# A three-network kernel on one core: the prologue rewritten, odd row tiles stored with 128 rows

## The chip, the cores and the metric

The kernel runs on one core of one Trainium2 chip. The metric is device time in microseconds (us) of one launch; the median of several runs counts.

The core has five engines that run at once and wait for one another by semaphores: PE (matmul; PEld is its weight load), DVE (vector), ACT (activation), POOL (GpSimd) and SP, which here does nothing but issue DMA transfers. Each engine takes its instructions in program order, so an instruction that waits holds up all that stand behind it on its engine.

## What is computed

Three networks in a row, all in float32 with some split into two parts of lower precision (a high and a low part) that are multiplied apart:

```python
kv = np.einsum('bhsd,bhse->bhde', k, v)            # 8 batches, 8 heads, 576 x 64
out = np.einsum('bhsd,bhde->bhse', q, kv)
out = out / np.sqrt(np.mean(out * out, -1, keepdims=True) + 1e-06) * g_norm
x = heads of out side by side                       # 8 x 576 x 512
u = x + real(fft(fft(x, axis=1), axis=2))
un = (u - mean) / sqrt(var + 1e-06)                 # over the last axis
x = u + max(un @ w1a, 0) @ w2a                      # 512 -> 2048 -> 512
u = x + (x.T @ U @ V).T                             # over the 576 rows, rank 32
return u + max(u @ w1b, 0) @ w2b
```

The weights come as 64-bit words that the kernel itself turns into float32 ("conversion" below).

## The kernel before

**Stages.** `tile_fused_kernel` is written in program order (`manual_schedule`), so the order of the code is the order on every engine. The *prologue* (L1232 to the line `early.clear()`) does batch 0 up to its normalised, transposed rows. Then come nine times 16 steps `n` of the first two-layer network: *block* j = n // 16 holds 512 rows, and the steps of block j also carry batch j + 1 through the attention, the DFT and the stores (`batch_tasks`, by step). The rest, from step 144, is a fast matrix product for the second network, which the change doesn't touch.

**A step of block 0.** `emit_l1(n)` is 12 matmuls of 128x512 (L223 to L225, with the weight's high part `w1h` and low part `w1l`), then come the eight passes of `emit_l2(n - 1)` (L244, needs the activation `g` of the step before). In the first block the steps also convert the weights: `w_load` (L102) starts a 512 KB transfer into one of four raw buffers, `w_mags` (`conv_0`, L113 and L114, ACT) takes it apart, `conv_a` (L122, L123) and `conv_b` (L128, L130) make the float32 tile on DVE, for every second tile with L130 on POOL. `w_next` then loads into the buffer that `conv_b` has just read. `split_w1` makes `w1h` on ACT (L198) and `w1l` on POOL (L199), or on DVE for steps in `on_dve`. ACT takes `w_mags` ahead of the next `g`.

**The prologue's path.** `load_first` brings k, v and q of batch 0 in two halves of four heads. `t_kv` multiplies k and v, `t_o0` multiplies by q half by half and takes the squares and sums (ten half tiles), `t_norm` scales. `t_fold_s`, `t_fold_e`, `t_fold_h`, `t_fold_l` fold the rows for a half-size DFT, `c` being one of three row chunks, `p` the even or odd part. `t_s1` is the DFT over the rows (PE, then `t_s1_out`: high part `y` on ACT, low part `y` on DVE), `t_s2` the DFT over the columns, three chunks in the order 2, 0, 1, each with seven DVE or ACT operations behind it that leave u in `x`. `f_stats` and `f_rs` make the mean and the reciprocal deviation, `f_norm` the normalised rows, `f_tr` the transpose into `xh` and `xl`, which `emit_l1(0)` reads. `keep_warm(n)` is n matmuls of 128x128 on the identity.

**Stores.** `t_u_out(b, c)` stores u to memory, two transfers for each chunk: the even rows (L549; 128, 128, 33 of them) and the odd rows (L551; 127, 128, 32: the first of chunk 0 is left out, since row 288 is an even one). The SP engine issues all transfers of the kernel in program order; a transfer's issue waits until the one eight places before it in the round has ended.

Of the kernel before, what the change touches and what calls it, by code (L numbers as in the profile page):

```python
# [45 lines left out]
def kernel(ctx: ExitStack, tc: tile.TileContext, qT, kvm, gn, w1a, w2a, w1b, w2b,  # L46
# [354 lines left out]
    def t_o0(k, half):  # L401
        s = st[0]
        g, c, m = OT[k]
        if k + half == 0:
            s["x"] = at.tile([C, 2, 3, DM], F32, tag="xpn", name="x0")
            s["sq"] = at.tile([C, 5, DM], F32, tag="slot_b", name="sq0")
            s["ss"] = whole(at, [C, 5, H], F32, "ss0", "ss", 2)
        ps = side_bank(f"o0_{k}_{half}")[:m, 0:256]
        cols, hs = slice(256 * half, 256 * half + 256), slice(4 * half, 4 * half + 4)
        for j in range(2):  # L410
            nc.tensor.matmul(out=ps[:, 128 * j:128 * j + 128], lhsT=s["q"][:, 2 * half + j, C * k:C * k + m],
                             rhs=kvbd[:, 2 * half + j, :], start=True, stop=True)
        sq = s["sq"][:m, k, cols]
        nc.scalar.activation(out=sq, in_=ps, func=AF.Square)
        heads = lambda v: v.rearrange("p (h d) -> p h d", d=D)
        nc.vector.tensor_tensor(out=heads(s["x"][:m, g, c, cols]), in0=heads(ps),
                                in1=gnb[:m].unsqueeze(1).to_broadcast([m, 4, D]), op=ALU.mult)
        ss = s["ss"][:m, k, hs]
        nc.vector.reduce_sum(out=ss, in_=heads(sq), axis=AX.X)
        nc.vector.tensor_scalar(out=ss, in0=ss, scalar1=1.0 / D, scalar2=EPS, op0=ALU.mult, op1=ALU.add)  # L420
        nc.gpsimd.tensor_tensor(out=ss, in0=ss, in1=nhalf[:m, 0:4], op=ALU.pow)

    def t_norm(b, k):
        s = st[b]
        g, c, m = OT[k]
        xv = s["x"][:m, g, c].rearrange("p (h d) -> p h d", d=D)
        rs = s["ss"][:m, k]
        if b == 1 or b == 0 and k in (1, 3):
            for h in range(8):
# [128 lines left out]
    def load_first():  # L558
        kv = at.tile([128, 2, KC, DM], F32, tag="slot_a", name="kv0")
        q = whole(at, [128, 4, NQ], F32, "q0", "slot_c")  # L560
        for half in range(2):
# [3 lines left out]
            if half == 0:
                nc.sync.dma_start(out=gnb, in_=gn)
            j = slice(2 * half, 2 * half + 2)
            nc.sync.dma_start(out=q[:, j], in_=qT[0][:, j])
# [662 lines left out]
    with tc.manual_schedule():  # L1231
# [20 lines left out]

        keep_warm(15)
        t_kv(0, 0)
        t_o0(0, 0)
        t_o0(1, 0)
        t_kv(0, 1)
        for k in range(2, 5):
            t_o0(k, 0)
        for k in range(5):  # L1260
            t_o0(k, 1)
        keep_warm(40)
        for k in (0, 1, 3):
            t_norm(0, k)
        for p in range(2):
            for c in range(3):
                t_fold_s(0, c, p)
                t_fold_e(0, c, p)
                t_fold_h(0, c, p)
                if p and c < 2:  # L1270
                    round_table(2, c)
                if p == 0:
                    if c == 0:
                        round_table(0, 0)
                    if c < 2:
                        t_norm(0, 2 * c + 2)
                if c:
                    t_fold_l(0, c - 1, p)
            t_fold_l(0, 2, p)
            round_table(2 - (not p), 2 * p)  # L1280
            if p == 0:
                for e in range(2):
                    t_s1_mm(0, 0, e)
                t_kve_mm(1, 0)
        for e in range(2):
            t_s1_out(0, 0, e)
# [248 lines left out]
```

## Time and profile before

| | us |
|---|---|
| median of 3 runs | 1778.59 (1778.1 to 1779.77) |
| the profiled execution | 1778.37 |
| its span, first to last instruction | 1776.6 |
| PE busy | 1740.6 (98%) |
| DVE, ACT, POOL busy | 1179.6, 833.6, 466.7 |
| DMA, share of 16 engines (q1) | 53.5% |

PE is the engine that sets the time. What PE is not busy is read by stretches: the prologue ends, and the first matmul of step 0 starts, at 61.23 us; block 0 goes to about 192 us. The granted clock is given as a share of full speed, 1.00 for 2.4 GHz and 0.50 for 1.2 GHz, so a stretch between the two shows a mean. DMA share 0.06 is one of the 16 DMA engines.

### The profile page before, as it was taken

Reading aid. Unit: us, or ns where it says so; the run is one execution under the profiler, and the core shown is the slowest. Engines: PE = TensorE matmul, PEld = TensorE weight load, DVE = VectorE, ACT = ScalarE, POOL = GpSimd, SP = SyncE. Lnnn points to the kernel's source line nnn. Section 1 sums busy time; section 2 is a strip of 40 time slices with the busy share of each in tenths; the row PEclk is TensorE's granted clock in tenths of the full one; section 3 lists DMA queues with packets and bytes.
Section 4 is the critical chain, followed back from the end, with each engine's and each line's share of the span. In section 5 each row is a group of like instructions: output and inputs, shape, how many; then the busy total and the mean of one; then the engine's idle time right before and its main releaser. Section 6 shows DMA issues by size and latency. Waiting matters only on the chain.

```text
span 1776.6 us, 23224 instructions
## 1 busy us (share of the span) xinstructions
PE 1740.6 (98%) x8206; PEld 1427.1 (80%) x8206; DVE 1179.6 (66%) x1927; ACT 833.6 (47%) x1601; POOL 466.7 (26%) x368
## 2 busy tenths in 40 slices
PE   7898999999999999999999999999999999999999
PEld 7666688888888888888888878878888888888877
DVE  5687777868677686765676666448835863594285
ACT  5575344444444344343446564456445534552253
POOL 2164445464534545443322223000000000000000
PEclk9999999999999999999999999999999999999999
DMA  8554315051432505203368864767776776777675
GB/s 327 188 193 148 127 36 195 6 183 54 157 135 96 174 24 206 86 20 114 102 234 307 312 224 168 233 175 247 239 241 182 236 257 194 220 227 236 188 217 188
DMA packets 130292, 315.23 MB, mean 177 GB/s; under 512 B 20592, under 2 KB 23424, under 8 KB 128512
## 3 DMA queue, kind: packets, MB, share of 16 engines
q1 hardware_dynamic: 130176, 313.75, 53.5%
q8 instruction: 65, 1.06, 0.2%
q14 instruction: 51, 0.42, 0.1%
HBM read 238.83 MB, written 74.86 MB: 177 GB/s over the span
## 4 chain that ended last, share of the span: by engine, by line
PE 83%; DVE 3%; DMA 3%; ACT 1%; issue 0%; SPq 0%; POOL 0%; ACTq 0%; DVEq 0%; POOLq 0%
PE y L1129 10%; PE yy L1209 10%; PE h L225 7%; PE h L223 7%; PE h L224 6%; PE acc L252 6%; PE acc L254 6%; PE acc L253 6%; PE z L1209 5%; PE zz L1129 5%; PE w L1209 3%; PE z L1129 3%; PE o L383 2%; DMA raw<-in_w2b 1%; PE pt L825 1%; DVE w2l L209 1%
## 5 line engine op out<-in xcount | busy, mean ns | idle before, releaser
L199 POOL TENSOR_TENSOR w1l<-w,w1h 128x512 fp32r<-128x512 f32 x147 | 200.0, 1361 | 402.8 <-ACT w1h L198 384.9
L223 PE MATMUL h<-xl,w1h 128*128 128x512 f32 x576 | 231.9, 403 | 4.8 <-DVE xl L679 2.6
L225 PE MATMUL h<-xh,w1l 128*128 128x512 f32 x576 | 226.2, 393 | 2.3 <-POOL w1l L199 2.3
L224 PE MATMUL h<-xh,w1h 128*128 128x512 f32 x576 | 225.7, 392 | 0.0
L252 PE MATMUL acc<-w2h,gl 128*128 128x512 f32 x524 | 206.1, 393 | 0.2 <-DVE gl L233 0.2
L254 PE MATMUL acc<-w2h,gh 128*128 128x512 f32 x524 | 204.3, 390 | 0.0
L253 PE MATMUL acc<-w2l,gh 128*128 128x512 f32 x524 | 204.2, 390 | 0.0
L1129 PE MATMUL y<-xv,v 128*128 128x512 f32 x768 | 191.8, 395 | 2.7 <-ACT g L1066 2.7
L232 ACT ACTIVATE gh<-h 128x512 fp32r<-128x512 f32 x147 | 87.5, 595 | 222.9 <-PE h L225 220.7
L1066 ACT ACTIVATE g<-y 128x512 f32<-128x512 f32 x128 | 76.6, 598 | 211.5 <-PE y L1129 211.5
L1129 PEld LDWEIGHTS y<-xv,v 128*128 128x128 f32 x768 | 143.7, 188 | 38.2 <-ACT g L1066 4.5
L233 DVE SCALAR_TENSOR_TENSOR gl<-h,gh 128x512 fp32r<-128x512 f32 x147 | 100.7, 685 | 87.6 <-ACT gh L232 87.3
L209 DVE TENSOR_TENSOR w2l<-w,w2h 128x512 fp32r<-128x512 f32 x147 | 139.1, 946 | 27.1 <-ACT w2h L208 26.7
L223 PEld LDWEIGHTS h<-xl,w1h 128*128 128x128 f32 x576 | 108.8, 189 | 27.3 <-ACT w1h L198 2.8
L225 PEld LDWEIGHTS h<-xh,w1l 128*128 128x128 f32 x576 | 108.7, 189 | 27.0 <-POOL w1l L199 3.5
L224 PEld LDWEIGHTS h<-xh,w1h 128*128 128x128 f32 x576 | 108.9, 189 | 22.2 <-issue 1.7
L252 PEld LDWEIGHTS acc<-w2h,gl 128*128 128x128 f32 x524 | 98.4, 188 | 22.1 <-DVE gl L233 2.5
L254 PEld LDWEIGHTS acc<-w2h,gh 128*128 128x128 f32 x524 | 98.4, 188 | 20.5
L253 PEld LDWEIGHTS acc<-w2l,gh 128*128 128x128 f32 x524 | 98.5, 188 | 19.7
L198 ACT ACTIVATE w1h<-w 128x512 fp32r<-128x512 f32 x160 | 99.8, 624 | 26.2 <-DVE w L130 20.8
L208 ACT ACTIVATE w2h<-w 128x512 fp32r<-128x512 f32 x147 | 91.7, 624 | 34.3 <-PE acc L254 30.7
L1060 DVE TENSOR_TENSOR g<-zz,g 128x512 f32<-128x512 f32 x64 | 44.2, 691 | 93.1 <-ACT g L1066 80.1
(243 smaller groups left out, 3678.8 us busy)
## 6 DMA issues: line engine op xcount, KB each, us to landing
v<-wv_d SPq DMA_DIRECT2D x224, 512.0 KB, 3.9
wv_d<-vo SPq DMA_DIRECT2D x112, 256.0 KB, 2.7
kve<-in_kvm SPq DMA_DIRECT2D x40, 256.0 KB, 6.1
x_d<-x2o SPq DMA_DIRECT2D x36, 256.0 KB, 2.1
x2f<-x_d SPq DMA_DIRECT2D x36, 256.0 KB, 5.2
outT<-o SPq DMA_DIRECT2D x36, 256.0 KB, 2.9
q<-in_qT SPq DMA_DIRECT2D x7, 1220.0 KB
raw<-in_w1b SPq DMA_DIRECT2D x16, 512.0 KB
```

The lines of the kernel that those rows point to most:

```text
L198: nc.scalar.activation(out=ah, in_=a, func=AF.Copy)
L199: (nc.vector if n in on_dve else nc.gpsimd).tensor_tensor(out=al, in0=a, in1=f32(ah), op=ALU.subtract)
L209: nc.vector.tensor_tensor(out=cl, in0=c, in1=f32(ch), op=ALU.subtract)
L223: nc.tensor.matmul(out=h, lhsT=ah[:, kc, :], rhs=xl[:, kc, :], start=(kc == 0), stop=False)
L224: nc.tensor.matmul(out=h, lhsT=ah[:, kc, :], rhs=xh[:, kc, :], start=False, stop=False)
L225: nc.tensor.matmul(out=h, lhsT=al[:, kc, :], rhs=xh[:, kc, :], start=False, stop=(kc == 3))
L233: nc.vector.scalar_tensor_tensor(out=gl, in0=h, scalar=0.0, in1=f32(gh), op0=ALU.max, op1=ALU.subtract)
L252: nc.tensor.matmul(out=a, lhsT=gl[:, tt], rhs=ch, start=s, stop=False)
L253: nc.tensor.matmul(out=a, lhsT=gh[:, tt], rhs=cl, start=False, stop=False)
L254: nc.tensor.matmul(out=a, lhsT=gh[:, tt], rhs=ch, start=False, stop=e)
L1129: nc.tensor.matmul(out=dst, lhsT=w[:, c], rhs=r[:, k], start=p in (0, 1, 3) and k + n == 0, stop=k == 1 and n == 2, skip_group_check=True)
L1209: nc.tensor.matmul(out=dst[mp], lhsT=w[:, c], rhs=r, start=p in (0, 1, 6, 3) and i + n == 0, stop=i == 7 and n == 2, skip_group_check=True)
```

## The change

- `t_o0` is gone. Batch 0 uses `t_o`, as the others do, over whole heads (five tiles); `load_first` brings k and v in halves, then q whole.
- Weight tile 0: `one(0)` (its conversion) and `split_w1(0)` no longer stand among `t_s1` and `t_s2`. `conv_a` now stands between the third and the fourth `f_norm`, `conv_b` behind the last one, the split behind `f_tr`. `w_load(0)` is issued with the other raw loads.
- The fold's order is written out. The `t_norm` of tile 2 goes to ACT, that of tile 3 to DVE; `y` of part 0 is split into `t_s1_hi`, placed inside the fold of part 1, and `t_s1_lo`, behind it. The second `keep_warm` has 60 matmuls, not 40.
- `f_stats(0)` goes behind the stats of tiles 1 and 2; `f_norm` of tiles 3 and 4 goes to DVE, and their two bias operations fall away.
- `t_u_out`: the odd rows of chunk 0 are stored with 128 rows. The one row too many is row 288, which the store of chunk 2 writes later. This holds for all eight batches. In the prologue chunks 0 and 1 are stored ahead of `kv_load_early(3, 6)`, and only chunk 2 at the old place, behind the raw loads.

```diff
-        if b == 1 or b == 0 and k in (1, 3):
+        if b == 1 or b == 0 and k in (1, 2):
...
-        n0, n1 = max(C * c, 1), min(C * c + C, 288)
+        n0, n1 = C * c, min(C * c + C, 288)
         nc.sync.dma_start(out=u_d[b][288 + n0:288 + n1, :], in_=s["x"][n0 - C * c:n1 - C * c, 1, c])
...
+        if i < 3:
+            nc.scalar.activation(out=un[0][i][:m], in_=x, func=AF.Identity, bias=first["b"][:m, i],
+                                 scale=first[1][:m, i])
+        else:
+            nc.vector.tensor_scalar(out=un[0][i][:m], in0=x, scalar1=first[2][:m, i, 0:1], scalar2=first[1][:m, i],
+                                    op0=ALU.subtract, op1=ALU.mult)
...
-        keep_warm(40)
-        for k in (0, 1, 3):
+        keep_warm(60)
+        for k in range(3):
             t_norm(0, k)
...
-        w_mags(0)
-        t_s1(0, 1, 0)
-        one(0)
-        t_s1(0, 1, 1)
+            t_s1_lo(0, 0, e)
+            round_table(2, 1 + e)
+        for e in range(2):
+            t_s1(0, 1, e)
         t_s2(0, 2)
         t_kve_out(1, 0)
-        on_dve.add(0)
-        split_w1(0)
         t_s2(0, 0)
-        f_stats(0)
         t_s2(0, 1)
+        w_mags(0, 1, 2, 3)
         load_q(1)
-        w_mags(1, 2, 3)
-        for i in (1, 2):
+        for i in (1, 2, 0):
             f_stats(i)
...
+        for c in range(2):
+            t_u_out(0, c)
         kv_load_early(3, 6)
...
-        for i in range(5):
+        for i in range(3):
             f_norm(i)
+        a0 = conv_a(raws.pop(0), w_new(0), pws.pop(0))
+        for i in (3, 4):
+            f_norm(i)
+        conv_b(*a0)
+        w_next((0,))
         for i in range(5):
             f_tr(i)
+        on_dve.add(0)
+        split_w1(0)
         one(2)
         split_w1(1)
         one(1)
-        for c in range(3):
-            t_u_out(0, c)
+        t_u_out(0, 2)
```

DVE between the two DFTs, before: `cv` and `w` are the conversion of weight tile 0, `y` the low parts, `de` the first operations of `t_s2`.

```order
L518 TENSOR_TENSOR y_452<-s_0_0_1_462,y_452 128x290
L518 TENSOR_TENSOR y_452<-s_0_1_0_506,y_452 128x290
L122 TENSOR_SCALAR cv_503<-cv_503 128x512
L123 TENSOR_SCALAR w_0_0_516<-cv_503 128x512
L128 SCALAR_TENSOR_TENSOR cv_503<-raw 128x512
L130 ISA w_0_0_516<-w_0_0_516,cv_503 128x1024
L518 TENSOR_TENSOR y_452<-s_0_1_1_523,y_452 128x290
L536 TENSOR_TENSOR de_2_547<-s_0_2_0_533,de_2_547 34x258
```

The same place now, with the line numbers of the changed file:

```order
L502 TENSOR_TENSOR y_440<-s_0_0_1_450,y_440 128x290
L502 TENSOR_TENSOR y_440<-s_0_1_0_492,y_440 128x290
L502 TENSOR_TENSOR y_440<-s_0_1_1_502,y_440 128x290
L520 TENSOR_TENSOR de_2_526<-s_0_2_0_512,de_2_526 34x258
L521 TENSOR_TENSOR de_2_526<-s_0_2_0_512,de_2_526 34x258
```

The four conversion instructions are gone from between the last two `y`. DVE at the prologue's end, before, from the last operations of `f_rs` (`first`) to `xl`:

```order
L653 TENSOR_SCALAR firstb<-first_238 128x2
L654 TENSOR_SCALAR first_239<-first_238 128x2
L679 TENSOR_TENSOR xl_709<-ftr_710,xh_708 128x4x33
L679 TENSOR_TENSOR xl_709<-ftr_717,xh_708 128x4x128
L679 TENSOR_TENSOR xl_709<-ftr_724,xh_708 128x4x127
L679 TENSOR_TENSOR xl_709<-ftr_731,xh_708 128x4x128
L679 TENSOR_TENSOR xl_709<-ftr_738,xh_708 128x4x96
```

And now, `cv` and `w` being the conversion of weight tile 0 and `un` the `f_norm` of tiles 3 and 4:

```order
L122 TENSOR_SCALAR cv_580<-cv_580 128x512
L123 TENSOR_SCALAR w_0_0_686<-cv_580 128x512
L653 TENSOR_SCALAR un_681<-x_283,first_237,first_238 128x512
L653 TENSOR_SCALAR un_681<-x_283,first_237,first_238 96x512
L128 SCALAR_TENSOR_TENSOR cv_580<-raw 128x512
L130 ISA w_0_0_686<-w_0_0_686,cv_580 128x1024
L668 TENSOR_TENSOR xl_696<-ftr_697,xh_695 128x4x33
L668 TENSOR_TENSOR xl_696<-ftr_704,xh_695 128x4x128
L668 TENSOR_TENSOR xl_696<-ftr_711,xh_695 128x4x127
L668 TENSOR_TENSOR xl_696<-ftr_718,xh_695 128x4x128
L668 TENSOR_TENSOR xl_696<-ftr_725,xh_695 128x4x96
L199 TENSOR_TENSOR w1l_733<-w_0_0_686,w1h_732 128x512
```

Four conversion instructions and two `un` now stand between `f_rs` and the five `xl`, and the split of weight tile 0 behind them. The transfers on SP at the prologue's end, before (`raw`, `more_raw`: the four raw weight buffers; `u_d`: the stores of u):

```order
L365 DMA kv_d_134<-kvr_678 64x256 x2
L102 DMA more_raw<-in_w1a 128x1024
L102 DMA raw<-in_w2a 128x1024
L549 DMA u_d_84<-x_271 128x512
L551 DMA u_d_84<-x_271 127x512
L549 DMA u_d_84<-x_271 128x512
L551 DMA u_d_84<-x_271 128x512
L549 DMA u_d_84<-x_271 33x512
L551 DMA u_d_84<-x_271 32x512
L102 DMA more_raw<-in_w2a 128x1024
L102 DMA raw<-in_w1a 128x1024
```

And now (four stores of 128 rows stand ahead of the ten `kve` loads, ahead of these rows):

```order
L365 DMA kv_d_134<-kvr_658 64x256 x2
L102 DMA raw<-in_w1a 128x1024
L102 DMA more_raw<-in_w1a 128x1024
L102 DMA raw<-in_w2a 128x1024
L533 DMA u_d_84<-x_283 33x512
L535 DMA u_d_84<-x_283 32x512
L102 DMA more_raw<-in_w2a 128x1024
```

No transfer of 127 rows is left in the program.

## Rows read from the trace of the kernel before

**Rows 1.** Three stretches: us, busy of each engine, PEclk, DMA share, GB/s.

```profile
0.00:61.20 61.20, 48.65 (x364) 45.49 (x364) 38.20 (x105) 35.30 (x84) 13.30 (x20) 0.94 0.82 303
61.20:192.00 130.80, 117.27 (x496) 82.74 (x497) 97.87 (x166) 73.34 (x165) 63.17 (x51) 0.96 0.54 174
192.00:1776.60 1584.60, 1574.67 (x7348) 1298.89 (x7346) 1043.51 (x1657) 724.93 (x1352) 390.21 (x298) 1.00 0.53 173
```

**Rows 2.** Stretches of 2 us, same columns.

```profile
70.00:72.00 2.00, 2.00 (x12) 1.67 (x12) 0.27 (x1) 0.33 (x1) 1.29 (x1) 1.00 0.06 16
...
86.00:88.00 2.00, 1.81 (x2) 0.84 (x3) 1.77 (x3) 2.00 (x5) 0.12 (x1) 0.55 0.25 47
```

**Rows 3.** A stretch of 0.5 us: PEclk, DMA share, GB/s.

```profile
72.00:72.50 0.50, 1.00 0.06 25
```

**Rows 4.** Timeline of SP's queue: start, us, issue.

```profile
66.90 0.32 SPq L551 DMA_DIRECT2D u_d<-x  x1
...
75.86 5.96 SPq L365 DMA_DIRECT2D kv_d<-kvr  x2
...
159.06 3.65 SPq L102 DMA_DIRECT2D raw<-in_w1a  x1
```

**Rows 5.** Timeline of block 0: start, us, operation, [idle before <- releaser].

```profile
84.29 0.66 ACT L113 ACTIVATE cv<-more_raw 128x512 f32<-128x512 f32 x1 [8.54 <-DMA more_raw<-in_w2a]
...
86.19 5.38 PE L244 MATMUL acc<-w,g 128*128 128x512 f32 x8 [5.18 <-ACT g L228]
...
95.93 3.60 PE L244 MATMUL acc<-w,g 128*128 128x512 f32 x8
...
140.39 0.40 PE L495 MATMUL s<-tab,e 97*128 97x290 f32 x1 [3.63 <-DVE e L483]
...
172.05 0.66 ACT L113 ACTIVATE cv<-raw 128x512 f32<-128x512 f32 x1 [7.70 <-DMA raw<-in_w1a]
...
175.41 0.50 PE L223 MATMUL h<-xl,w1h 128*128 128x512 f32 x1 [2.16 <-ACT w1h L198]
176.84 0.50 PE L225 MATMUL h<-xh,w1l 128*128 128x512 f32 x1 [0.70 <-POOL w1l L199]
...
184.91 0.50 PE L225 MATMUL h<-xh,w1l 128*128 128x512 f32 x1 [1.59 <-POOL w1l L199]
```

**Rows 6.** Timeline of the prologue.

```profile
23.20 0.68 DVE L432 TENSOR_TENSOR x<-x,ss 128x512 f32<-128x512 f32 x1
...
39.63 0.42 DVE L122 TENSOR_SCALAR cv<-cv 128x512 f32<-128x512 f32 x1
...
41.88 0.45 DVE L518 TENSOR_TENSOR y<-s,y 128x290 fp32r<-128x290 f32 x1
...
42.39 0.43 PE L531 MATMUL s<-tab,y 128*34 128x258 f32 x1 [2.07 <-DVE y L518]
...
45.71 0.67 DVE L199 TENSOR_TENSOR w1l<-w,w1h 128x512 fp32r<-128x512 f32 x1
...
54.78 0.16 DVE L654 TENSOR_SCALAR first<-first 128x2 f32<-128x2 f32 x1
...
58.83 2.35 DVE L679 TENSOR_TENSOR xl<-ftr,xh 128x512 fp32r<-128x512 f32 x4 [0.19 <-ACT xh L678]
...
61.23 0.50 PE L223 MATMUL h<-xl,w1h 128*128 128x512 f32 x1 [2.62 <-DVE xl L679]
```

**Rows 7.** Durations: keep_warm(40), two rows a matmul; whole heads in batch 1.

```profile
18.80 9.10 PE L399 MATMUL warm<-ident 128*128 128x128 f32 x80
...
89.45 0.69 DVE L387 TENSOR_TENSOR x<-o,gnb 128x512 f32<-128x512 f32 x1 [1.65 <-ACT sq L385]
...
90.85 0.69 DVE L387 TENSOR_TENSOR x<-o,gnb 128x512 f32<-128x512 f32 x1
```

**Rows 8.** One line's durations, ns min/median/max: a normalisation on DVE.

```profile
L694 DVE TENSOR_SCALAR un<-un,ln,ln x32: 536/544/549, 192.6 to 848.2; 128x512 f32<-128x512 f32 x32
```

**Rows 9.** DMA issues of the page: count, KB each, us to landing.

```profile
x_d<-x2o SPq DMA_DIRECT2D x36, 256.0 KB, 2.1
```

More of the change, by code (lines that the diff above doesn't have):

```diff
@@ L399, in keep_warm @@
             nc.tensor.matmul(out=ps[:, 0:128], lhsT=ident, rhs=ident, start=True, stop=True)
[L401 to L421, printed above, removed]
     def t_norm(b, k):
@@ L564, in load_first @@
                 nc.sync.dma_start(out=kv[:, a, :, c], in_=kvm[0][:, a, :, c])
[L565 to L568, printed above, removed]
+        nc.sync.dma_start(out=q, in_=qT[0])
+        nc.sync.dma_start(out=gnb, in_=gn)
         st[0] = {"kv": kv, "q": q}
@@ L652, in f_rs @@
         rs, nb = first[1][:, a:b], first["b"][:, a:b]
-        nc.vector.tensor_scalar(out=nb, in0=first[2][:, a:b, 0:1], scalar1=-1.0, scalar2=None, op0=ALU.mult)
+        if a == 0:
+            nc.vector.tensor_scalar(out=nb, in0=first[2][:, a:b, 0:1], scalar1=-1.0, scalar2=None, op0=ALU.mult)
         nc.vector.tensor_scalar(out=rs, in0=first[2][:, a:b, 1:2], scalar1=EPS, scalar2=None, op0=ALU.add)
         nc.gpsimd.tensor_tensor(out=rs[:, :, 0], in0=rs[:, :, 0], in1=nhalf[:, 0:b - a], op=ALU.pow)
-        nc.gpsimd.tensor_tensor(out=nb, in0=nb, in1=rs, op=ALU.mult)
+        if a == 0:
+            nc.gpsimd.tensor_tensor(out=nb, in0=nb, in1=rs, op=ALU.mult)
     def f_norm(i):
@@ L663, in f_norm @@
             un[0].insert(0, z.rearrange("p a b -> p (a b)")[:, 0:DM])
-        nc.scalar.activation(out=un[0][i][:m], in_=st[0]["x"][:m, g, c], func=AF.Identity,
-                             bias=first["b"][:m, i], scale=first[1][:m, i])
+        x = st[0]["x"][:m, g, c]
+        if i < 3:
[4 more added lines that the diff above has]
+                                    op0=ALU.subtract, op1=ALU.mult)
     def f_tr(i):
@@ L1241 @@
         load_table(2)
-        w_load(0)
         kv_load_early(2, 11)
-        for k in (1, 2, 3):
+        for k in range(4):
             w_load(k)
@@ L1254 @@
         t_kv(0, 0)
-        t_o0(0, 0)
-        t_o0(1, 0)
         t_kv(0, 1)
-        for k in range(2, 5):
-            t_o0(k, 0)
         for k in range(5):
-            t_o0(k, 1)
-        keep_warm(40)
-        for k in (0, 1, 3):
+            t_o(0, k)
+        keep_warm(60)
+        for k in range(3):
             t_norm(0, k)
-        for p in range(2):
-            for c in range(3):
[L1267 to L1284, printed above, removed]
@@ L1285 @@
-        for e in range(2):
-            t_s1_out(0, 0, e)
-        w_mags(0)
-        t_s1(0, 1, 0)
-        one(0)
-        t_s1(0, 1, 1)
+        t_fold_s(0, 0, 0)
+        t_fold_e(0, 0, 0)
+        t_fold_h(0, 0, 0)
+        t_norm(0, 3)
+        round_table(0, 0)
+        t_fold_s(0, 1, 0)
+        t_norm(0, 4)
+        t_fold_e(0, 1, 0)
+        t_fold_h(0, 1, 0)
+        t_fold_l(0, 0, 0)
+        t_fold_s(0, 2, 0)
+        t_fold_e(0, 2, 0)
+        t_fold_h(0, 2, 0)
+        t_fold_l(0, 1, 0)
@@ new lines @@
+        t_fold_l(0, 2, 0)
+        for e in range(2):
+            t_s1_mm(0, 0, e)
+        t_kve_mm(1, 0)
+        round_table(1, 0)
+        for c in range(2):
+            t_fold_s(0, c, 1)
+            t_fold_e(0, c, 1)
+            if c:
+                t_s1_hi(0, 0, 0)
+            t_fold_h(0, c, 1)
+            if c:
+                t_s1_hi(0, 0, 1)
+                t_fold_l(0, 0, 1)
+            else:
+                round_table(2, 0)
+        t_fold_s(0, 2, 1)
+        t_fold_e(0, 2, 1)
@@ L1291 @@
+        t_fold_h(0, 2, 1)
+        t_fold_l(0, 1, 1)
+        t_fold_l(0, 2, 1)
+        for e in range(2):
+            t_s1_lo(0, 0, e)
+            round_table(2, 1 + e)
+        for e in range(2):
+            t_s1(0, 1, e)
         t_s2(0, 2)
         t_kve_out(1, 0)
-        on_dve.add(0)
-        split_w1(0)
         t_s2(0, 0)
-        f_stats(0)
         t_s2(0, 1)
+        w_mags(0, 1, 2, 3)
         load_q(1)
-        w_mags(1, 2, 3)
-        for i in (1, 2):
+        for i in (1, 2, 0):
@@ L1306 @@
         t_kv_early(1, 1)
+        for c in range(2):
+            t_u_out(0, c)
         kv_load_early(3, 6)
```

7 lines of the change are left out of this document (5 added, 2 removed).

## The prediction

> **What bounds the kernel now.** First the three stretches [rows 1]: behind 192 us PE is busy for 1574.67 of 1584.60 us at full clock, so nothing off PE can bring more than a few us there. Ahead of that PE is idle 12.55 us in the prologue and 13.53 us in block 0. So I read the prologue's last path and block 0's stalls; the change touches only these, apart from one more row in seven later stores.
>
> Block 0's stalls [rows 5]: PE waits 5.18 us at 86.19 for `g`, which ACT makes late because it stood 8.54 us before a raw weight load (`more_raw`) landed; it waits 3.63 us at 140.39 for DVE in batch 1's DFT; and 2.16, 0.70 and 1.59 us from 175.41 to 184.91 for split weights, behind an ACT wait of 7.70 us, again for a raw load. Both ACT waits have one picture in the DMA rows. At 66.90 SP issues the store of odd rows, chunk 0, with 127 rows [rows 4]. From 70 to 72 us the DMA engines are busy for 0.06 of their time at 16 GB/s [rows 2], at 72.0 with 0.06 at 25 GB/s [rows 3]: that is one engine of 16. 127 rows of 2 KB are 260 KB, at 25 GB/s 10.4 us. What is issued behind it has its sixteenth on the same engine and can't end sooner; and since a transfer waits for the one eight places ahead, the queue stands too: 5.96 us for `kv_d` at 75.86 [rows 4], which holds back the next raw load. Batch 1's store of this kind comes just ahead of 159.06, where the next raw load's issue takes 3.65 us [rows 4]. For a store of 128 rows the nearest row is `x_d`: 256 KB land in 2.1 us [rows 9].
>
> The prologue ends at 61.23 with the last `xl` [rows 6]. Its path runs from the data over DVE (23.20) to the second DFT (PE waits 2.07 us for a `y` at 42.39), three chunks of DVE work, `f_rs` (54.78), `f_norm`, transposes, `xl`.
>
> **The change part by part**, against the profiled execution (1778.37 us, of it 1776.6 span; the median 1778.59 is 0.2 above).
>
> *Stores of 128 rows.* The one-engine transfer goes, so the first raw load lands like the others. PE's 5.18 us go, and what they cost afterwards: the eight matmuls behind them took 5.38 instead of 3.60 us [rows 5], the granted clock being at 0.55, a mean between 2.4 and 1.2 GHz, after the idle time [rows 2]. That is 5.18 + 1.78 = 6.96. ACT, DVE and POOL were all waiting on the same load, so nothing else is late next: POOL's split for the following step has the lead it had. In batch 1: 2.16 + 0.70 + 1.59 = 4.45. The three waits are one: DVE and POOL do the work of two steps close together once the load is there. Bounds: of the 6.96 at least 5.18; of the 4.45 at least 2.86 (the last one could be POOL's own pace); no loss, since the extra row is 2 KB on a queue that is then shorter. Value: 6.96 + 4.45 = 11.4. In batches 2 to 7 the same clog is there and PE is full [rows 1]: 0.
>
> The Trainium skill, DMA: Bandwidth & Descriptors, section "Why a DMA increments its semaphore by 16 and not by 1", says that a DMA is spread over the largest number of engines up to 16 that divides its slowest dimension, with 127 partitions on one. Rows 3 agree (0.06, 25 GB/s). By that rule the stores of 128 and 32 rows use all 16 engines and that of 33 rows 11, and the sum stays as it is; were the slowness that of any store here, the 11.4 would be 0 (third rival).
>
> *Earlier stores, later raw loads.* Four stores (1.05 MB) now stand ahead of the ten `kve` loads, with q's 1.25 MB: 4.9 MB from about 44 us. The prologue's mean is 303 GB/s at a share of 0.82, so 370 when full [rows 1]: until 57 to 60 us. PE needs `kve` behind step 0's 12 matmuls, at 62. The next raw load (tile 4) now waits for the late `conv_b`, lands near 60, and ACT comes to it at 61 to 62. Cost 0; up to 2 us if DMA runs at 303.
>
> *Heads whole.* Ten half tiles become five whole ones of 1.40 us on DVE (90.85 - 89.45, [rows 7]), 7.0 us. q now lands behind all of k and v, with 3.9 MB at about 14.5 us, DVE starts near 16.3 and the norm follows at 23.3, against 23.20 [rows 6]: +0.1 (-1 to +1.5).
>
> *60 instead of 40 warm matmuls.* One takes 9.10/40 = 0.23 us [rows 7], 20 take 4.55. PE has 20 products with q (4.6 us by the same rate) from 14.5 us on and is then warm until 32.8; the DFT of part 0 and a `kve` product (4.4 us at full clock) end at 37.3, where they ended at about 36.9 with waits and half clock in between. Cost 0.4 (0 to 4.5). The new fold order gives DVE up to 0.8 us, which this covers.
>
> *Weight tile 0 out of the DFTs.* The last `y` goes from 41.88 to behind its high part, in place of the conversion that began at 39.63 [rows 6]: -2.25. With the 0.4 above the second DFT starts 1.9 earlier. Behind it 0.6 of `w1l` (45.71, 0.67 with overlap) goes. `f_rs` ends at 54.94 - 1.9 - 0.6 = 52.4.
>
> *What is added at the end.* On DVE, two operations of 0.43 (`conv_a`), two `f_norm` like L694 (0.544, [rows 8]), then `conv_b`, 2.25 - 0.86 = 1.4: 3.35 in all, until 55.8. Then `xl`, 2.35 for four tiles [rows 6] and about 0.25 for the first: 58.4. ACT isn't later: three `f_norm` of 0.8 instead of five follow the reciprocal at about 52. Step 0 starts at 58.4 instead of 61.23, -2.8; its third matmul needs `w1l` (0.67 behind `xl`; two matmuls of 0.23 run first), +0.2. So -2.6 (bounds 0 and -4.5).
>
> *The wait at 140.39* remains: ACT, DVE and POOL hold one another up there, no store does. 0; down to -5.5 (3.63, and the clock's loss behind, 1.78 by the nearest row).
>
> Sum: 6.96 + 4.45 + 2.6 = 14.0. 1778.4 - 14.0 = 1764.4; on the median's scale 1764.6.
>
> **The rivals.**
> 1. *The engines get ahead.* With raw loads in time ACT and DVE could gain a lead over PE that also eats the wait at 140.39. For: their work comes as early as PE lets it. Against: a raw load follows the conversion that frees its buffer, so there is little room for a lead. It would give 1764.6 - 5.4 = 1759.2, at most; 0.17.
> 2. *The prologue gains nothing.* 60 warm matmuls and the DVE block ahead of `xl` are what the end waits for, with later data. For: DVE goes without a gap from `f_rs` to `xl`. Against: 2.07 us of PE wait had no other cause than the conversion. 1767.2; 0.12.
> 3. *The clog isn't the row count.* Then the stores are as slow with 128 rows, the stalls stay, and only the prologue's 2.6 is left: 1776.0, within 0.2%. Against: `x_d`, and one engine of 16 at work. 0.04.
> 4. *Slower.* `w_mags` of tiles 0 to 3 stand on ACT ahead of the `kve` copies and `f_norm`; raw tile 0 now comes behind 11.8 MB. If it landed late, ACT and then everything would stop there. ACT comes to it at about 44 us; 11.8 MB take 32 us (at 370 GB/s) to 39 us (at 303), so it is in time by 4 us or more. To end 3.6 us above the old time it would have to land at 44 + 14 + 4 = 62 us: 1782 and more; 0.03.
>
> **How the numbers follow.** The forecast 1764.6 with 0.64, the rivals with 0.17, 0.12, 0.04 and 0.03. About 0.2% (3.6 us) is what a measurement of this kernel can tell from no change. The forecast's own bounds: down by 1.9 in the prologue, up by 1.8 + 1.6 if the clock's loss and the last POOL wait stay. The range goes from 1758, which takes in most of rival 1, to 1769.5, which takes in rival 2 with a small loss. Faster: 0.64 + 0.17 + 0.12 = 0.93; same 0.04; slower 0.03.
>
> **What would show it.** Right: step 0's first matmul near 58.4; no stretch at DMA share 0.06 with 25 GB/s behind the stores of chunk 0; no PE wait of 5 us some 25 us into block 0, none of 2 us near its end; ACT's waits for raw loads under 2 us; PE from step 16 on as busy as before. Wrong: the first matmul at 61 or later with DVE full up to it (rival 2); no PE wait in batch 1's DFT (rival 1); the stall in step 2 still there behind the same raw load (rival 3); ACT idle at 44 us behind raw tile 0 (rival 4). A new wait of PE in block 0 on split weights would mean that POOL or DVE, not the loads, sets the pace.

## The result and the profile after

| us | before | after |
|---|---|---|
| median | 1778.97 (1778.1 to 1779.77) | 1760.38 (1760.04 to 1761.43) |
| ratio, 95% interval | | 0.9897 (0.9879 to 0.9914) |
| the profiled execution, its span | 1778.37, 1776.6 | 1760.34, 1758.4 |

The change makes the kernel 18.6 us faster: 1760.4 against 1764.6 forecast, inside the range, 4.2 us below the forecast. The three stretches of [rows 1] with the kernel after in place of the one before, cut at the same times (us, busy time of PE, PEld, DVE, ACT and POOL, granted clock, DMA share, GB/s):

```profile
0.00:61.20 61.20, 53.77 (x422) 51.45 (x423) 41.40 (x97) 34.22 (x78) 12.20 (x15) 0.97 0.90 324
61.20:192.00 130.80, 126.93 (x557) 90.82 (x556) 103.68 (x176) 79.09 (x176) 65.53 (x53) 0.97 0.53 181
192.00:1758.40 1566.40, 1557.05 (x7272) 1286.05 (x7270) 1035.09 (x1641) 718.65 (x1340) 386.06 (x295) 1.00 0.53 174
```

PE is busy 9.7 us longer in the same 130.8 us of block 0 (126.93 against 117.27) and 5.1 us longer in the first 61.2 us, where the 20 more warm matmuls alone make up some 4.6. (The same work stands up to 17 us earlier in the second trace, so the stretches hold it in part only.) All PE waits of over 0.15 us from 56 to 192 us, of the kernel before and then of the kernel after (line, what it waited for, us in total, times, longest):

```profile
PE acc L244 <- ACT g L228: 5.2, 1, 5.2
PE s L495 <- DVE e L483: 3.6, 1, 3.6
PE h L223 <- DVE xl L679: 2.6, 1, 2.6
PE h L225 <- POOL w1l L199: 2.3, 2, 1.6
PE h L223 <- ACT w1h L198: 2.2, 1, 2.2
PE ftr L674 <- ACT un L664: 0.3, 1, 0.3
```

```profile
PE s L473 <- DVE e L461: 3.9, 1, 3.9
PE h L223 <- DVE xl L668: 2.7, 1, 2.7
```

The first, fourth and fifth of the kernel before, the ones that the prediction laid to the 127-row stores, are gone (the last one, at 0.3, now lies before 56 us). Two stay, one in batch 1's first DFT and one ahead of step 0. The timeline of the kernel after at the places of [rows 4 to 6] (start, us, operation, [idle before <- releaser]; SPq is the issuing queue):

```profile
56.46 0.77 PE L223 MATMUL h<-xl,w1h 128*128 128x512 f32 x1 [2.71 <-DVE xl L668]
...
71.39 0.66 ACT L113 ACTIVATE cv<-more_raw 128x512 f32<-128x512 f32 x1
...
75.78 3.59 PE L244 MATMUL acc<-w,g 128*128 128x512 f32 x8
...
128.41 0.61 PE L473 MATMUL s<-tab,e 97*128 97x290 f32 x1 [3.87 <-DVE e L461]
...
147.48 0.33 SPq L102 DMA_DIRECT2D raw<-in_w1a  x1
...
167.25 0.79 PE L223 MATMUL h<-xl,w1h 128*128 128x512 f32 x1
```

ACT, which had waited 8.54 us for the eighth raw tile (84.29 in [rows 5]), takes the same tile at 71.39 without a wait; its longest wait for a raw tile in block 0 is now one of 2.45 us at 104.64, and no wait of PE follows from it. The eight matmuls L244 that had waited 5.18 start at 75.78 without a wait and take 3.59 instead of 5.38, and SP's issue behind batch 1's store takes 0.33 us instead of 3.65 [rows 4].

Read as the distance between the same instruction in the two traces, the gain came thus:

| place in the program (before, after) | earlier by | what that stretch gave | forecast |
|---|---|---|---|
| step 0's first matmul (61.23, 56.46) | 4.8 | 4.8 | 2.6 |
| `kve` behind step 0 (65.65, 60.62) | 5.0 | 0.3 | 0 |
| the `L244` behind the stalled one (95.93, 83.73) | 12.2 | 7.2 | 6.96 |
| L223 behind batch 1's first DFT (153.81, 142.23) | 11.6 | -0.6 | 0 |
| the first `o` of block 1 (204.87, 188.01) | 16.9 | 5.3 | 4.45 |
| the last 45 matmuls (1761.59, 1743.46) | 18.1 | 1.3 | 0 |

The two profiled executions are 18.0 us apart, the medians 18.6.

### The profile page after: what moved, and what is told of

Same layout as the page of the kernel before. It is cut to its first block, busy times and chain, and to the rows that moved or that the text cites. A ratio compares the mean times of both kernels' runs of the same rounds, so it can differ in the third digit from the quotient of the medians.

```text
span 1758.4 us, 23273 instructions
## 1 busy us (share of the span) xinstructions
PE 1737.7 (99%) x8246; PEld 1428.3 (81%) x8246; DVE 1180.2 (67%) x1913; ACT 832.0 (47%) x1594; POOL 463.8 (26%) x362
## 4 chain that ended last, share of the span: by engine, by line
PE 93%; DMA 3%; DVE 2%; ACT 1%; issue 1%; SPq 0%; POOL 0%; ACTq 0%; DVEq 0%; POOLq 0%
PE y L1118 10%; PE yy L1198 10%; PE h L223 8%; PE h L225 8%; PE h L224 8%; PE acc L252 7%; PE acc L254 7%; PE acc L253 7%; PE z L1198 5%; PE zz L1118 5%; PE w L1198 3%; PE z L1118 3%; PE o L383 2%; PE pt L814 1%; PE acc L244 1%; PE u L839 1%
## 5 line engine op out<-in xcount | busy, mean ns | idle before, releaser
L223 PE MATMUL h<-xl,w1h 128*128 128x512 f32 x576 | 232.0, 403 | 2.7 <-DVE xl L668 2.7
L225 PE MATMUL h<-xh,w1l 128*128 128x512 f32 x576 | 226.0, 392 | 0.0
L223 PEld LDWEIGHTS h<-xl,w1h 128*128 128x128 f32 x576 | 109.1, 189 | 24.9 <-issue 4.1
L225 PEld LDWEIGHTS h<-xh,w1l 128*128 128x128 f32 x576 | 108.7, 189 | 24.4 <-POOL w1l L199 0.6
```

The source lines that it names most:

```text
L223: nc.tensor.matmul(out=h, lhsT=ah[:, kc, :], rhs=xl[:, kc, :], start=(kc == 0), stop=False)
L225: nc.tensor.matmul(out=h, lhsT=al[:, kc, :], rhs=xh[:, kc, :], start=False, stop=(kc == 3))
```

## Experiments

Every experiment ran beside runs of the kernel before on the same chip, whose medians were 1779.2 to 1779.4. The half-width of the ratios' intervals is 0.1 to 0.2%, some 2 to 3 us; differences below that rest on the traces, one execution of each kernel.

### Are the stores the cause, and each of its own stall?

One line undone in the kernel after:

```diff
-        n0, n1 = C * c, min(C * c + C, 288)
+        n0, n1 = max(C * c, 1), min(C * c + C, 288)
```

> The changed kernel with one line of it undone: the odd half's first tile is stored from row 1 on again, 127 rows, in all eight batches. Theory: the two clogs are worth what the markers of the two traces shift by in the two places, 7.1 us in step 2 and 5.3 us at the end of block 0, together 12.4, and the prologue's share stays: 1760.4 + 12.4 = 1772.8. Rival (the stores are innocent, something else in the change removed the stalls): no stall, 1760.4. Rival (an earlier prologue only fills up the wait behind the clog, so that it is worth nothing while the clog stands): 1778 to 1779. In the trace, by the theory: a PE wait of about 5 us in step 2 behind the second raw tile, and a stretch of about 10 us in which the DMA engines are busy for 0.06 of their time.

Measured: 1774.55 (1773.37 to 1775.61), ratio 0.9971 (0.9960 to 0.9982): a loss of 14.2 us against the kernel after, not 12.4, and it didn't arise where I expected it. PE and ACT of that kernel, and the stretch of 2 us behind the store of chunk 0:

```profile
64.80 7.85 PE L348 MATMUL kve<-kve,kve 128*128 128x128 f32 x40 [3.40 <-DMA kve<-in_kvm]
...
69.79 0.66 ACT L113 ACTIVATE cv<-raw 128x512 f32<-128x512 f32 x1 [9.54 <-DMA raw<-in_w1a]
...
168.13 0.66 ACT L113 ACTIVATE cv<-raw 128x512 f32<-128x512 f32 x1 [7.69 <-DMA raw<-in_w1a]
```

```profile
58.00:60.00 2.00, 2.00 (x6) 1.52 (x5) 1.90 (x5) 0.39 (x1) 0.00 (x0) 0.50 0.08 31
```

The DMA engines are at 0.08 with 31 GB/s, as in [rows 2, 3]. The low share doesn't last the 10 us of the expectation: it shows in two stretches of about 2.5 us, from 49.0 and from 58.0, with other transfers between them. But the change also moves this store ahead of the ten `kve` loads, so now these stand behind it, and PE waits for a `kve` load (3.40) right behind step 0, not in step 2. The eight-matmul wait in step 2 doesn't return, against the expectation's last sentence. 127 rows at the new place would have been dearer than at the old one. The second stall, at 168.13, is the old one (7.70 in [rows 5], 7.69 here).

The same line alone, in the kernel before (the reverse edit):

> The kernel before with the one line of the change: 128 rows in the odd half's first tile, in all batches. Theory: 1779.0 - 12.4 = 1766.6, and what the whole change has beyond that, about 6, is the prologue's. Rival (stores innocent): 1779.0. Rival (the stores gain only with the prologue, whose stores of the first two tiles stand earlier): 1772 to 1777, with part of the wait in step 2 still there.

Measured: 1766.67 (1766.17 to 1767.37), ratio 0.9928 (0.9913 to 0.9943). One row more in each of eight stores gives 12.7 us of the 18.6, all the rest of the change some 6. Neither stall is there any more; step 0's first matmul stands at 61.37, where it was. ACT gets the eighth raw tile nearly at once:

```profile
76.15 0.70 ACT L113 ACTIVATE cv<-more_raw 128x512 f32<-128x512 f32 x1 [0.24 <-DMA more_raw<-in_w2a]
```

The stores were guilty, and by themselves. Which of the eight?

```diff
-        n0, n1 = C * c, min(C * c + C, 288)
+        n0, n1 = max(C * c, b == 0), min(C * c + C, 288)
```

> The changed kernel with 127 rows in batch 0's store alone. Theory (each clog has its own store): the wait in step 2 comes back, the one at the end of block 0 doesn't: 1760.4 + 7.1 = 1767.5. Rival (the second stall is a late echo of the first): both come back, 1772.8. Rival (the first clog is taken up by the slack of later waits): under 1764.

The same with `b == 1`:

> The changed kernel with 127 rows in batch 1's store alone. Theory: only the stall at the end of block 0 comes back, 1760.4 + 5.3 = 1765.7. Rival (the second stall is an echo of the first): 1760.4. What the run with 127 rows in all batches has beyond this one's loss and batch 0's is the price of the stores of batches 2 to 7; theory: 0 to 1, since PE waited for nothing behind them in either trace.

Measured: 1768.89 (1768.41 to 1769.36) with batch 0's store slow, 8.5 us; 1766.01 (1765.38 to 1766.86) with batch 1's, 5.6 us. Batch 0's has the `kve` wait and no second stall, batch 1's the second stall and no `kve` wait. PE in the first, then in the second of the two kernels:

```profile
65.02 8.08 PE L348 MATMUL kve<-kve,kve 128*128 128x128 f32 x40 [3.68 <-DMA kve<-in_kvm]
```

```profile
163.94 0.50 PE L223 MATMUL h<-xl,w1h 128*128 128x512 f32 x1 [2.32 <-ACT w1h L198]
...
165.36 0.50 PE L225 MATMUL h<-xh,w1l 128*128 128x512 f32 x1 [0.69 <-POOL w1l L199]
...
173.44 0.50 PE L225 MATMUL h<-xh,w1l 128*128 128x512 f32 x1 [1.63 <-POOL w1l L199]
```

Neither is an echo of the other. The 8.5 can be counted: the forty `kve` matmuls start 4.4 us later than in the kernel after (65.02 against 60.62) and take 8.08 instead of 4.63, since the clock is at 0.50 to 0.56 from 64 to 70 us behind the wait: 4.4 + 3.45 = 7.9. The two losses add up to 14.1, and all eight slow stores cost 14.2, so the medians show no price for the stores of batches 2 to 7. The traces show a small one, within the 0 to 1 that was expected. From 250 to 400 us, the part of the program with the stores of batches 2 and 3, the kernel before falls back by another 0.6 us against the kernel after (from 16.8 to 17.4), and so does the kernel with 127 rows in all batches (from 12.75 to 13.39), each time 0.2 to 0.3 where PE's transposes `tr` wait for DVE's `un`. With 127 rows in batch 0 or batch 1 alone, and in the kernel before with 128 rows, the distance there stays within 0.04.

### The count of rows, or the row that the store begins at?

The slow store differs from the good one in two ways: it has 127 rows, and it begins at row 1. Two kernels part these. The first stores rows 0 to 126 and row 127 apart (below); the second begins at row 1 and cuts at row 113, 112 and 15 rows:

```diff
-        n0, n1 = C * c, min(C * c + C, 288)
-        nc.sync.dma_start(out=u_d[b][288 + n0:288 + n1, :], in_=s["x"][n0 - C * c:n1 - C * c, 1, c])
+        n0, n1 = max(C * c, 0), min(C * c + C, 288)
+        for a, z in (((n0, 127), (127, n1)) if c == 0 else ((n0, n1),)):
+            nc.sync.dma_start(out=u_d[b][288 + a:288 + z, :], in_=s["x"][a - C * c:z - C * c, 1, c])
```

> The changed kernel, the odd half's first tile stored as rows 0 to 126 (127 rows from row 0) and row 127 alone. What made the store slow: the count of rows, or that it began at row 1? Theory (the count): a store of 127 rows again takes one DMA engine and about 10 us, both stalls come back, 1774.6 as with 127 rows from row 1. Rival (the start at row 1 in the tile and in memory): 1760.4, no stall.

> The changed kernel, the odd half's first tile stored from row 1 on in two pieces of 112 and 15 rows. Theory (the count of rows): 112 is 16 x 7 and 15 divides into 15 engines, so both pieces land in 1 to 3 us, no stall, 1760.4 with one more issue for each batch (up to 0.5). Rival (the start at row 1): both stalls, 1774.6.

Measured: 1773.7 (1772.51 to 1774.86) with 127 + 1 rows, 1762.2 (1760.94 to 1762.47) with 112 + 15. The stretch from 58 to 60 us of the first, then of the second:

```profile
58.00:60.00 2.00, 1.54 (x7) 0.94 (x5) 1.90 (x4) 0.63 (x1) 0.09 (x1) 1.00 0.07 26
```

```profile
58.00:60.00 2.00, 2.00 (x14) 1.76 (x12) 1.90 (x5) 0.63 (x1) 0.13 (x1) 1.00 1.07 411
```

And the two stalls of the first, the first of them again behind step 0:

```profile
64.57 7.25 PE L348 MATMUL kve<-kve,kve 128*128 128x128 f32 x40 [5.03 <-DMA kve<-in_kvm]
...
171.13 0.60 PE L223 MATMUL h<-xl,w1h 128*128 128x512 f32 x1 [2.09 <-ACT w1h L198]
```

0.07 of the engines with 127 rows that begin at row 0, 1.07 with 112 that begin at row 1 (a transfer's time is counted in the stretch where it begins, so a share can pass 1): it is the count. The 1.8 us of the second over the kernel after lie within the intervals; its trace has no stall, only a wait of 0.17 us for a `kve` load and one of 0.2 for a split weight.

### What the prologue is made of

Weight tile 0 as before the change, its load ahead of the early `kve` loads, its conversion and split on DVE among the DFTs; all else as in the kernel after:

```diff
+        w_load(0)
         kv_load_early(2, 11)
-        for k in range(4):
+        for k in (1, 2, 3):
             w_load(k)
...
-        for e in range(2):
-            t_s1(0, 1, e)
+        w_mags(0)
+        t_s1(0, 1, 0)
+        one(0)
+        t_s1(0, 1, 1)
         t_s2(0, 2)
         t_kve_out(1, 0)
+        on_dve.add(0)
+        split_w1(0)
         t_s2(0, 0)
         t_s2(0, 1)
-        w_mags(0, 1, 2, 3)
+        w_mags(1, 2, 3)
...
-        a0 = conv_a(raws.pop(0), w_new(0), pws.pop(0))
         for i in (3, 4):
             f_norm(i)
-        conv_b(*a0)
-        w_next((0,))
         for i in range(5):
             f_tr(i)
-        on_dve.add(0)
-        split_w1(0)
```

> The changed kernel with weight tile 0 as it was: loaded ahead of the early k and v tiles, converted and split on DVE among the DFTs, not at the end. Theory (DVE is full from the second DFT to the first matmul, so that the place of the conversion decides only what stands beside idle time): the last statistic comes 2.4 + 0.7 later, and 2.4 of that is saved at the end, so the first matmul of step 0 comes at 57.0 to 57.6 instead of 56.46, 1760.9 to 1761.6. Rival (the conversion's move is the prologue's main gain, as the forecast had it): the first matmul at 59 or later, 1763 and more.

Measured: 1763.06 (1762.3 to 1764.7), ratio 0.9907 (0.9892 to 0.9922). Here my theory fell and its rival held: step 0's first matmul stands at 59.10, not at 57.0 to 57.6. PE's wait in the second DFT and the stretches behind it, of this kernel:

```profile
41.39 0.31 PE L515 MATMUL s<-tab,y 128*34 128x258 f32 x1 [2.07 <-DVE y L502]
```

```profile
40.00:42.00 2.00, 0.61 (x5) 0.59 (x6) 1.30 (x3) 0.02 (x1) 0.00 (x0) 1.00 0.39 100
42.00:44.00 2.00, 2.00 (x14) 2.00 (x13) 1.61 (x5) 1.46 (x5) 0.00 (x0) 0.64 0.42 166
44.00:46.00 2.00, 2.00 (x11) 2.00 (x11) 2.00 (x6) 0.34 (x1) 0.00 (x0) 0.51 0.00 0
```

And of the kernel after:

```profile
42.00:44.00 2.00, 2.00 (x21) 2.00 (x20) 2.00 (x7) 1.43 (x4) 0.00 (x0) 1.00 0.32 59
44.00:46.00 2.00, 2.00 (x20) 2.00 (x19) 2.00 (x7) 2.00 (x5) 0.00 (x0) 1.00 0.92 321
```

The wait of 2.07 us, the one in [rows 6], is back to the hundredth, and behind it the clock is at 0.64 and 0.51 for four microseconds, where the kernel after has 1.00. `kve` behind the DFT starts at 46.16 instead of 42.32, 1.2 us of it by the clock.

But that is not what the theory had wrong. On DVE its first half came true: the last statistic (L637) comes at 53.40 instead of 50.44, 2.96 later for the 2.4 + 0.7 expected. Its second half didn't: of the 2.4 that were to be saved at the end only 0.3 were. DVE of this kernel ahead of step 0:

```profile
54.38 1.00 DVE L653 TENSOR_SCALAR un<-x,first,first 128x512 f32<-128x512 f32 x2 [0.81 <-POOL first L638]
56.22 0.30 DVE L668 TENSOR_TENSOR xl<-ftr,xh 128x132 fp32r<-128x132 f32 x1 [0.84 <-ACT xh L667]
56.70 2.35 DVE L668 TENSOR_TENSOR xl<-ftr,xh 128x512 fp32r<-128x512 f32 x4 [0.19 <-ACT xh L667]
```

With the conversion taken away DVE is idle there for 1.84 us, waiting for POOL and ACT. In the kernel after the conversion fills that time, so at the end it costs next to nothing, and among the DFTs it costs its full length. The low clock adds 0.66 at most: it delays `kve`, whose copies hold up the first `f_norm` on ACT, which starts at 53.65 though POOL had its last input at 52.97.

Next, 40 warm matmuls instead of 60:

```diff
-        keep_warm(60)
+        keep_warm(40)
```

> The changed kernel with 40 warm matmuls instead of 60 ahead of the first DFT. Theory (the 20 more keep the clock up over the wait for the fold, and so earn more than they cost): the granted clock falls to 0.5 to 0.7 somewhere between 31 and 46 us, the second DFT ends 1 to 2 us later, 1761 to 1762.5. Rival (they only cost, as the forecast had it with 0.4): the first DFT starts earlier by up to 0.4, 1760.0. Second rival (the DFT doesn't wait for them at all): 1760.4.

Measured: 1759.01 (1757.57 to 1761.78), ratio 0.9885 (0.9870 to 0.9900). The theory fell: from 28 to 60 us the granted clock is 1.00 throughout. The first DFT starts at 27.21 instead of 31.53, so PE in the kernel after is held up by its own warm matmuls. It then waits for the fold, 0.90 us at 28.75 and 0.46 and 0.34 further on, and step 0 starts at 54.79, 1.67 earlier. (So the low clock of the kernel before in the second DFT came from the conversion's wait, not from too few warm matmuls.) But of the 1.67 nothing is left in this profiled execution (1761.78, the slowest of the four, which lie 4.2 us apart): at 103 us PE is level with the kernel after, 0.04 ahead. Its ACT and PE, then ACT of the kernel after at the same instruction:

```profile
74.81 0.68 ACT L113 ACTIVATE cv<-raw 128x512 f32<-128x512 f32 x1 [2.11 <-DMA raw<-in_w2a]
...
77.83 1.16 PE L383 MATMUL o<-kvbd,q 128*128 128x128 f32 x8 [1.39 <-DVE x L387]
```

```profile
74.80 0.67 ACT L113 ACTIVATE cv<-raw 128x512 f32<-128x512 f32 x1 [0.40 <-DMA raw<-in_w2a]
```

ACT gets to the raw tile 1.7 us earlier and waits 1.7 us longer: it lands at the same 74.8. DVE's work behind ACT, and PE behind DVE, then come no earlier. Why it lands no earlier, though it was issued earlier (69.83 against 71.51), wasn't tried.

The heads in halves again (`t_o0`, ten half tiles, q in two pieces, as before the change):

```diff
         t_kv(0, 0)
+        t_o0(0, 0)
+        t_o0(1, 0)
         t_kv(0, 1)
+        for k in range(2, 5):
+            t_o0(k, 0)
         for k in range(5):
-            t_o(0, k)
+            t_o0(k, 1)
...
```

> The changed kernel with the heads in halves as before: q in two pieces, the products, squares, sums and powers of each tile in two halves (10 pairs instead of 5). Theory (the whole heads give what the first fold's marker gained, and PE's 60 warm matmuls hide it): the normalisation comes 0.75 later, the first DFT still starts behind the warm matmuls and by them 0 to 0.8 later; first matmul of step 0 at 56.5 to 57.3, 1760.4 to 1761.2. Rival (whole heads are much of the prologue's gain): 2 us and more later, 1762.5. Second rival (halves let PE start on the half of k and v that lands first, and are better): under 1760.

Measured: 1763.17 (1761.36 to 1764.88), ratio 0.9908 (0.9893 to 0.9923). By the median this is the rival's figure, by the trace (an execution of 1761.36) the theory's: step 0 starts at 56.65, 0.19 later, and the end of block 0 is 0.2 later too, the clock behind step 0's wait being low for longer in between. The two don't agree and the intervals overlap, so I leave the price of the halves at 0.2 to 2.8.

### Can the clock that is lost behind the two remaining waits be had?

Behind the wait ahead of step 0 the clock of the kernel after is at 0.50 and 0.67 for 4 us, behind the one in batch 1's DFT at 0.50 for 6 us. Warm matmuls in the waits should keep it up:

```diff
         for i in range(5):
             f_tr(i)
+        keep_warm(20)
```

> The changed kernel with 20 warm matmuls (2.4 us at 0.12 each) in PE's wait of 2.71 us ahead of step 0. Theory (that wait lets the clock fall to 0.50 and 0.67 for the next 4 us, which costs 1.4 to 1.7): the clock stays 1.00 and step 0 ends 1.4 to 1.7 earlier, 1758.7 to 1759.0. Rival (the loads of the k and v tiles that PE multiplies next, issued just before, land too late for it): PE waits for a DMA there instead, 1760.4.

and in the DFT (for batch 1, part 0, first half only):

```diff
+        if s_warm[0]:
+            s_warm[0] = False
+            keep_warm(30)
         if p == 0:
             nc.tensor.matmul(out=out, lhsT=z288, rhs=tb["z288"], start=False, stop=False)
...
```

> The changed kernel with 30 warm matmuls (3.6 us) in PE's wait of 3.87 us inside batch 1's first DFT, ahead of the matmul that waits. Theory (the wait and the clock's loss behind it are two losses, and the second can be had alone): the clock stays at 1.00 where it was 0.50 for 6 us, the DFT's ten matmuls and step 11's first seven go at 0.14 and 0.23 instead of 0.25 and 0.43, 2.7 less: 1757.7. Rival (what made the wait, the lead of ACT, DVE and POOL, makes the next one as well, and PE only waits later): 1760.4.

Measured: 1760.18 (1759.97 to 1760.72) and 1761.11 (1760.88 to 1761.67): no gain. Both edits were sized wrongly: a warm matmul shows as two rows of 0.115 us ([rows 7] say so), so the pieces lasted 4.4 and 6.86 us, beyond the waits of 2.71 and 3.87. So both once more at half the size, 10 and 15, in one kernel:

> The changed kernel with both of the last two edits at half their size, since one warm matmul of 32-bit data shows as two of 0.115 and the pieces of 20 and 30 were twice as long as the waits: 10 (2.3 us) ahead of step 0 and 15 (3.4 us) inside batch 1's first DFT. Theory (the clock's loss behind the two waits can be had alone, 1.6 at step 0 and 2.7 at the DFT, if the warm matmuls end before the wait does): the clock at 1.00 from 50 to 62 us and from 124 to 137 us, 1756.1 to 1757.5. Rival (PE is ahead of ACT, DVE and POOL in block 0, and what it gains at one place it waits for at the next): 1759.5 to 1760.5, with a longer wait in the DFT or a new one of 1 to 2 us after it.

Measured: 1759.56 (1759.3 to 1759.77), ratio 0.9887 (0.9871 to 0.9904). The clock is at 1.00 everywhere, as the theory wanted, and yet only 0.8 us come of the 4.3 that it promised. PE of this kernel:

```profile
56.43 0.47 PE L223 MATMUL h<-xl,w1h 128*128 128x512 f32 x1 [0.45 <-DVE xl L674]
59.36 4.63 PE L348 MATMUL kve<-kve,kve 128*128 128x128 f32 x40
...
103.08 2.39 PE L348 MATMUL kve<-kve,kve 128*128 128x128 f32 x20
...
124.17 3.51 PE L399 MATMUL warm<-ident 128*128 128x128 f32 x30
...
133.80 0.40 PE L469 MATMUL s<-tab,eh 128*128 128x290 f32 x1 [1.46 <-DVE y L508]
```

and of the kernel after:

```profile
60.62 4.63 PE L348 MATMUL kve<-kve,kve 128*128 128x128 f32 x40
...
103.16 2.39 PE L348 MATMUL kve<-kve,kve 128*128 128x128 f32 x20
```

PE leaves step 0 1.26 us earlier, and at 103 us it is level again: 0.08. In the DFT the warm matmuls move the next half forward, where PE waits 1.46 us for `y`, a wait that the kernel after doesn't have. That is the rival: PE's gain up to 103 us is lost to the others, in three pauses too short for the list of waits: 0.4 us among the `o` from 77.97 on (for DVE's `x`), 0.24 ahead of the L244 at 96.40 (ACT's `g`) and 0.35 around the L225 at 100.65 (POOL's `w1l`). What holds these three engines back there wasn't tried. Of all versions tried this one and the one with 40 warm matmuls have the lowest medians, 0.8 and 1.4 us under the kernel after, within the intervals.

## Why the prediction held, and where it was off

**The first stall, 6.96 forecast, 7.2 found.** Cause, place and price were right, the price from PE's wait and the clock's loss behind it. The line alone gives 12.7 us in the kernel before against the forecast's 11.4 for both stalls. The Trainium skill, DMA: Bandwidth & Descriptors, section "Why a DMA increments its semaphore by 16 and not by 1", lets a DMA run on the largest number of engines up to 16 that divides its slowest dimension; by that rule 127 rows get one engine wherever they begin, 112 get 16 and 15 get 15. The shares of 0.07 and 1.07 in the two runs agree, so the third rival (0.04) is out.

**The second stall, 4.45 forecast, 5.3 to 5.6 found.** I added up three named waits of PE. Batch 1's slow store alone cost 5.6 us, the markers move by 5.3. The waits leave out what each of them breaks up: matmuls of this kind start 0.23 us apart when they are fed, but the one ahead of a wait takes its whole 0.39, and the one behind it 0.34 until the next. That is 0.27 for each of the three waits, 0.8 in all, and 4.45 + 0.8 is the 5.3. The clock was 1.00 there.

**The prologue, 2.6 forecast, 4.8 found: the mis-sized term.** It lies outside the bounds of 0 to 4.5 as well; that the sum stayed in the range is owed to the lower end that was set for the first rival. The step that failed is the second DFT "1.9 earlier", and in it the cost of 0.4 for the warm matmuls. DVE of the kernel before (first row) and of the kernel after:

```profile
43.69 0.42 DVE L536 TENSOR_TENSOR de<-s,de 34x258 f32<-34x258 f32 x1 [1.36 <-ACT de L535]
```

```profile
38.53 0.46 DVE L502 TENSOR_TENSOR y<-s,y 128x290 fp32r<-128x290 f32 x1 [0.47 <-ACT y L498]
...
40.04 0.42 DVE L520 TENSOR_TENSOR de<-s,de 34x258 f32<-34x258 f32 x1 [1.04 <-ACT de L519]
...
50.44 0.17 DVE L637 TENSOR_SCALAR first<-first 128x2 f32<-128x2 f32 x1
...
53.16 0.69 DVE L130 CUSTOM_DVE_ANT_0 w<-w,cv 128x1024 uint16<-128x1024 uint16 x1
```

The last `y` starts at 38.53 instead of 41.88 [rows 6], 3.35 earlier and not 1.9; the first `de` 3.65 earlier, the 0.3 more being the low clock behind PE's wait; the last `first` 4.34 earlier, with `w1l` gone from between; step 0 4.77. The tile's own 2.25 was well sized: undoing its move brings the last `y` 2.35 later. The rest is the DFT ahead of it. The forecast had it end 0.4 later, and it ends 0.8 earlier (its last matmul starts at 37.76 instead of 38.53). The products with q start at 13.69, not at 14.5, so the 60 warm matmuls end at 31.5 and not at 32.8; and the DFT of part 0 and the `kve` product behind them take 4.4 us as forecast, where they had taken 8.6 (28.11 to 36.70), with waits and 3.4 us at half clock. The low clock in the second DFT, which I had priced for the stall in step 2 and forgotten here, makes `kve` behind it 4.6 earlier where the DFT is 3.3, but step 0 hangs on DVE, and there it gives the 0.3.

By the runs the conversion's move is worth 2.64 at step 0's first matmul, which leaves 2.1 of the 4.8 for all else. In that the 60 warm matmuls cost 1.67 (0.4 was forecast: they, not the fold, release the first DFT) and whole heads give 0.2 or more, and so some 3.6 are left for the fold's new order, the two normalisations on DVE and the moved stores, which were not run apart; the sum takes it that the parts don't act on one another. The run with 40 warm matmuls, as many as before, shows 3.1 of it in the first DFT: part 1 of it starts at 33.64 instead of 36.70. The forecast took the order for "up to 0.8". What is added at the end was sized well: forecast 3.35 from `f_rs` to the end of `conv_b`, found 50.61 to 53.85 in the rows above, 3.2.

**The waiting DFT, 0 forecast, -0.6 found.** It stayed, 3.87 instead of 3.63 us, and the clock is low for longer behind it. The first rival (0.17), that the engines get ahead and eat it, is refuted: DVE's `e` comes 12.0 us earlier there, PE 12.2. The last run shows it from the other side.

**Cost nothing, as said.** The stores ahead of the `kve` loads, and the later raw loads: PE has no wait for a load in block 0, ACT waits 1.69 us for tile 4, under the 2 us named as a sign (one later wait, 2.45 us at 104.64, is over it). But that holds with 128 rows alone; with 127 the same order costs 8.5 us instead of 7.2. The fourth rival's late raw tile 0 didn't happen (ACT takes it at 42.85 without a wait), and the second rival, a prologue that gains nothing, is out with step 0 at 56.46.

**The last 1.3 us** were not forecast. They lie behind block 0. 0.5 come up to 400 us, and they are the price of the slow stores of batches 2 and 3 (above), which the prediction put at 0. The other 0.8 come between 850 and 1070 us, where neither the code nor the stores differ, and are luck: that part takes 220.0 us in the kernel after, 221.0 in the kernel before, 221.7 in the kernel before with 128 rows, and 220.0 to 221.4 in the others.

## What to carry to other kernels

Look at the row counts of transfers before their bytes: one store of 254 KB on one engine held up loads that had nothing to do with it, and one more row in each of eight such stores, written twice, was worth 12.7 us. Price a wait of PE together with the low clock behind it, but follow the price to the engine that the next stage waits for (1.2 us on PE were 0.3 at step 0 here), and don't count such a gain as final: in block 0 here the other engines took back what PE won. Warm matmuls are work on PE's queue and must end before the wait does.

## What the runs showed of the hardware

The clock doesn't fall alike after a wait of the same length. Ahead of step 0 PE waits 2.70 or 2.71 us in the kernel after and in seven of the kernels made from it, with the same products before it. In the kernel after the granted clock is at 0.50 in the 2 us from 56 on; with 127 rows in batch 1 alone it is at 0.93 there and at 0.50 only in the next 2 us; with 112 + 15 rows and with 40 warm matmuls it is 1.00 up to 62 us. The kernel with 112 + 15 rows leaves step 0 1.3 us earlier for it (59.30 against 60.62), and its span is no shorter (1759.2). Executions of one kernel differ as well: with weight tile 0 moved back the mean granted clock of its four runs is 0.996 to 0.999. So a price for the clock read from one trace is one draw.

Slow stores cost by what stands behind them. The same 127 rows cost 7.2 us behind the raw loads, 8.5 ahead of the `kve` loads, 5.6 at the end of block 0, 0.3 each in batches 2 and 3, and nothing that shows in the four behind them.
